# Fixed program order, phases, quadrant attention, DMA transposes and a Strassen second matmul in a sigmoid-attention + SiLU feed-forward kernel

## The chip, the cores and the metric

The kernel runs on one core of a Trainium2 chip. The metric is the time of one execution in microseconds (us) of the device. All quoted times are medians over the fast executions of a kernel (values_serial has one execution, of unknown state). Each kernel was run beside the kernel before on the same chip, and a ratio is the mean time of one kernel's fast runs over that of the kernel before's fast runs of the same rounds, so it is not quite the ratio of the medians quoted beside it. Experiments ran in four groups on four chips, so between groups the ratios are compared, not the times.

Short names: TensorE (PE in the profile) does matmuls, DVE is the vector engine, ACT the scalar engine (here: sigmoids), Pool is GpSimd, SP issues DMAs. SBUF is the on-chip memory, PSUM holds the results of matmuls, in banks. "Granted clock" is the share of full TensorE speed that the profile reports.

## The reference

Sigmoid attention for 8 batches of 12 heads (448 tokens, 64 values per head), followed by a two-matmul feed-forward block with SiLU over all 3584 tokens. Inputs and outputs are float32; both kernels multiply in float16.

```
q, k, v: (8, 12, 448, 64)   w_in: (768, 2048)   w_out: (2048, 768)
scores = q @ k^T / sqrt(64) - log(448)
x      = sigmoid(scores) @ v             # (8, 12, 448, 64) -> (3584, 768)
h      = x @ w_in                        # "first product"
out    = (h * sigmoid(h)) @ w_out        # "second product"
```

## The kernel before

It interleaves finely. For each pair of heads of batch b it issues the transposes of q and k on TensorE, four score blocks with their sigmoids and the values of the previous pair, and then one sixth of the feed-forward work of batch b - 1. A scheduler then orders the instructions; PSUM tiles come from two rotating pools. These are the parts that the change touches (cuts are marked):

```python
    def attention_part1(b: int, hp: int):
        # ... casting DMA loads of q16, k16, v16 (float32 -> float16) by the Pool queue ...
        for tsel, tin in ((0, q16), (1, k16)):
            ptr = ps_1.tile([P, 512], F32, ...)
            for c in range(NCH):            # 4 chunks of 112 tokens
                for j in range(2):          # 2 heads
                    nc.tensor.matmul(ptr[j*D:(j+1)*D, c*CP:(c+1)*CP],
                                     tin[:, j, c, :], ident[:CP, :CP], ...)   # a transpose, L94
            nc.vector.tensor_copy(qkT[:, tsel, :], ptr[:, :S])
        for c in range(NCH):
            # ... two score matmuls (one per head), one sigmoid, L107 and L114 ...

    def moe_out_unit(m, g):                 # second product: 128 tokens, L176
        for nh in range(2):                 # 2 x 384 output columns
            for fc in range(NFC - 1, -1, -1):        # 16 blocks of the inner dimension
                nc.tensor.matmul(po[:, :NO2], gTr[:, fc, g*P:(g+1)*P],
                                 w_out_sb[:, fc, nh*NO2:(nh+1)*NO2], ...)
            # ... DVE evacuates po with a scale into osb ...

    for b in range(B):
        for hp in range(NPAIR):
            va = attention_part1(b, hp)
            # ... values of the previous pair; some weights loaded ...
            if b > 0:
                moe_slice(b - 1, hp)        # a sixth of batch b-1's feed-forward work
```

## Time and profile before

| What | Before |
|---|---|
| Time, 3 runs | 490.87 us (490.77 to 491.74) |
| TensorE busy | 459.4 us of the span of 492.7 us of the profiled execution |
| First product (768 matmuls of 448 columns) | 1.14 us for six: 146 us |
| Second product (896 matmuls of 384 columns) | 2.60 us for sixteen: 146 us |
| Two transposes per head pair | 0.39 us each (median), 48 pairs |

From the profile page of the kernel before, four rows: busy microseconds with the share of the span and the number of instructions per engine; TensorE's busy tenths in 40 equal slices; the granted TensorE clock in tenths; and the shares of the chain of waits that ended last.

```profile
PE 459.4 (93%) x3200; PEld 227.7 (46%) x3200; DVE 184.1 (37%) x328; ACT 243.4 (49%) x321; POOL 124.7 (25%) x159
PE   3879999999999999999999999999999999999896
PEclk9985999999999999999999999999999999999999
PE 63%; ACT 25%; DVE 6%; DMA 2%; issue 2%; POOL 0%; ACTq 0%; POOLq 0%
```

A nine means 90% or more. From the fifth slice on (each is 12.3 us; the fourth is busy, but at a clock of 0.5) TensorE has work nearly all the time at full clock, and no other engine is busy for even half of the span. So the kernel is bound by the amount of work on TensorE, and only less work there, or denser work, can make it faster. ACT's quarter of the chain does not speak against it: TensorE's own waits for ACT add up to 6.8 us in the whole run.

The timeline of TensorE in the middle of the run prices that work. Columns: start, duration in us, engine, source line, operation, output and inputs, array tile, shapes, number of instructions, and in brackets the idle time before with what ended it.

```profile
231.21 0.39 PE L94 MATMUL ptr_2_0_2430<-ident,q_4_2_2423 112*64 112x112 f16 x8
231.55 0.39 PE L94 MATMUL ptr_2_1_2440<-ident,k_4_2_2424 112*64 112x112 f16 x8
232.32 0.96 PE L128 MATMUL pav_1_2467<-attnT_1_2356,v_4_1_2331 112*64 112x448 f16 x8 [0.38 <-DVE gTr L167]
235.75 0.40 PE L107 MATMUL psc_2_2_2459<-qkT_2_2429 64*112 64x448 f16 x2
236.08 0.55 PE L158 MATMUL ph_9_2487<-xT,w_in_sb 128*128 128x448 f16 x2
```

The first two lines are the two transposes of a head pair, 0.7 us together. `64*112` in the fourth line is the part of the 128x128 array that a score matmul uses, less than half of it; the two heads of a pair use the two halves. In the single records the two matmuls of a pair start 0.003 to 0.005 us apart. That line also shows a lone score pair amid the first product.

The chain of waits in order of time (start, duration, engine, tile, line) gives the pace and the ends:

```profile
171.09 2.42 ACT attnT_1_1758 L114 x3
286.47 2.42 ACT attnT_1_2992 L114 x3
448.00 1.29 PE ph_0_4713 L158 x6
```

The same tile of two later batches comes 115.4 us apart: 57.7 us per batch. The last batch's products begin at 448.0 us, with no attention beside them, and take the 44.7 us to the end of the span.

### The profile page before, as it was taken

The numbers are of one execution on the slowest core, as the hardware profiler recorded it, in microseconds if no ns is written. First come the engines' busy times: TensorE is split into PE (matmuls) and PEld (weight loads), VectorE is DVE, ScalarE is ACT, GpSimd is POOL, SyncE is SP. The second block draws the span as 40 slices with busy tenths as digits, with TensorE's granted clock in tenths as the row PEclk, the third lists the DMA queues.
The fourth block names the chain that finished last, engine by engine and source line by source line (L and its number), as shares of the span: only waits on it lengthen the run. The fifth ranks groups of instructions, "written<-read, shape, count | busy, mean of one in ns | idle before, by whom it ended". The sixth has DMA issues, their size and how long they took to land.

```text
span 492.7 us, 7595 instructions
## 1 busy us (share of the span) xinstructions
PE 459.4 (93%) x3200; PEld 227.7 (46%) x3200; DVE 184.1 (37%) x328; ACT 243.4 (49%) x321; POOL 124.7 (25%) x159
## 2 busy tenths in 40 slices
PE   3879999999999999999999999999999999999896
PEld 1333444544455444554455544454445544454463
DVE  2221453343622435226342353523533335324511
ACT  3665656347633575535743357427662275732400
POOL 9364231132301313113211131303321123000000
PEclk9985999999999999999999999999999999999999
DMA  9999975658456776764846666559483486211011
GB/s 89 168 169 189 179 51 37 92 63 55 29 60 93 72 45 44 73 93 31 55 29 93 92 46 41 60 64 85 30 57 75 83 57 39 18 59 40 0 56 73
DMA packets 140641, 34.30 MB, mean 70 GB/s; under 512 B 131904, under 2 KB 137024, under 8 KB 140608
## 3 DMA queue, kind: packets, MB, share of 16 engines
q0 software_dynamic: 136576, 22.82, 60.4%
q1 hardware_dynamic: 4032, 11.01, 5.9%
q8 instruction: 25, 0.41, 0.4%
q14 instruction: 8, 0.07, 0.0%
HBM read 45.61 MB, written 11.01 MB: 115 GB/s over the span
## 4 chain that ended last, share of the span: by engine, by line
PE 63%; ACT 25%; DVE 6%; DMA 2%; issue 2%; POOL 0%; ACTq 0%; POOLq 0%
DVE gTr L167 4%; DMA q_0_5_344<-in_q_dram 2%; ACT attnT_0_108 L114 1%; ACT attnT_1_1122 L114 1%; ACT attnT_1_2992 L114 1%; ACT attnT_1_4226 L114 1%; ACT attnT_1_2356 L114 1%; ACT attnT_1_1758 L114 1%; ACT attnT_1_3590 L114 1%; ACT attnT_1_521 L114 1%; DMA k_0_0_82<-in_k_dram 1%; PE pav_0_169 L128 1%; PE pav_4_388 L128 1%; PE po_3_0_4874 L176 1%; PE po_6_1_5006 L176 1%
## 5 line engine op out<-in xcount | busy, mean ns | idle before, releaser
L176 PEld LDWEIGHTS <-gTr 128*128 128x128 f16 x896 | 83.0, 98 | 68.3 <-issue 12.9
L158 PEld LDWEIGHTS <-w_in_sb 128*128 128x128 f16 x768 | 67.0, 98 | 81.2 <-issue 30.6
L114 ACT ACTIVATE attnT_0_2898<-psc_0_0_2899,bias_s 112x896 f16<-112x896 f32 x1 | 1.0, 1008 | 9.7 <-PE psc_0_0_2899 L107 9.7
L114 ACT ACTIVATE attnT_0_1028<-psc_0_0_1029,bias_s 112x896 f16<-112x896 f32 x1 | 1.0, 1008 | 9.7 <-PE psc_0_0_1029 L107 9.7
L114 ACT ACTIVATE attnT_0_1664<-psc_0_0_1665,bias_s 112x896 f16<-112x896 f32 x1 | 1.0, 1007 | 9.7 <-PE psc_0_0_1665 L107 9.7
L114 ACT ACTIVATE attnT_0_3496<-psc_0_0_3497,bias_s 112x896 f16<-112x896 f32 x1 | 1.0, 1007 | 9.7 <-PE psc_0_0_3497 L107 9.7
L114 ACT ACTIVATE attnT_0_2262<-psc_0_0_2263,bias_s 112x896 f16<-112x896 f32 x1 | 1.0, 1007 | 9.7 <-PE psc_0_0_2263 L107 9.7
L114 ACT ACTIVATE attnT_0_4132<-psc_0_0_4133,bias_s 112x896 f16<-112x896 f32 x1 | 1.0, 1007 | 9.7 <-PE psc_0_0_4133 L107 9.7
L114 ACT ACTIVATE attnT_5_1534<-psc_5_0_1535,bias_s 112x896 f16<-112x896 f32 x1 | 1.0, 1007 | 9.6 <-PE psc_5_0_1535 L107 9.6
L114 ACT ACTIVATE attnT_5_2768<-psc_5_0_2769,bias_s 112x896 f16<-112x896 f32 x1 | 1.0, 1007 | 9.6 <-PE psc_5_0_2769 L107 9.6
L114 ACT ACTIVATE attnT_5_4002<-psc_5_0_4003,bias_s 112x896 f16<-112x896 f32 x1 | 1.0, 1007 | 9.6 <-PE psc_5_0_4003 L107 9.6
L166 ACT ACTIVATE tsig_0_4720<-ph_0_4713 128x448 f16<-128x448 f32 x1 | 0.5, 544 | 10.5 <-PE ph_0_4713 L158 10.5
L114 ACT ACT_TABLE_LOAD x1 | 1.3, 1283 | 8.1 <-PE psc_0_0_109 L107 8.1
L94 PE MATMUL ptr_0_0_88<-ident,q_0_0_81 112*64 112x112 f16 x8 | 0.6, 299 | 4.6 <-DMA q_0_0_81<-in_q_dram 4.6
L176 PE MATMUL po_3_0_4874<-w_out_sb,gTr 128*128 128x384 f16 x16 | 2.8, 327 | 1.3 <-DVE gTr L167 1.3
L84 POOL DMA_DIRECT2D q_5_1_2965<-in_q_dram x1 | 0.8, 820 | 11.8 <-PE ptr_5_1_2758 L94 11.8
L84 POOL DMA_DIRECT2D q_7_1_4199<-in_q_dram x1 | 0.8, 820 | 11.8 <-PE ptr_5_1_3992 L94 11.8
L84 POOL DMA_DIRECT2D q_3_1_1731<-in_q_dram x1 | 0.8, 820 | 11.6 <-PE ptr_5_1_1524 L94 11.6
L84 POOL DMA_DIRECT2D q_6_2_3657<-in_q_dram x1 | 0.8, 820 | 11.4 <-PE ptr_0_1_3486 L94 11.4
L84 POOL DMA_DIRECT2D q_2_2_1189<-in_q_dram x1 | 0.8, 820 | 11.1 <-PE ptr_0_1_1018 L94 11.1
L84 POOL DMA_DIRECT2D q_3_2_1825<-in_q_dram x1 | 0.8, 820 | 11.1 <-PE ptr_0_1_1654 L94 11.1
L84 POOL DMA_DIRECT2D q_7_2_4293<-in_q_dram x1 | 0.8, 820 | 11.1 <-PE ptr_0_1_4122 L94 11.1
(1494 smaller groups left out, 1172.7 us busy)
## 6 DMA issues: line engine op xcount, KB each, us to landing
w_in_sb<-in_moe_w_in_dram POOLq DMA_DIRECT2D x4, 768.0 KB, 9.9
w_out_sb<-in_moe_w_out_dram POOLq DMA_DIRECT2D x4, 768.0 KB, 10.7
out_dram<-osb_0_833 SPq DMA_DIRECT2D x1, 384.0 KB, 2.9
out_dram<-osb_1_925 SPq DMA_DIRECT2D x1, 384.0 KB, 2.3
out_dram<-osb_2_963 SPq DMA_DIRECT2D x1, 384.0 KB, 2.4
out_dram<-osb_3_1431 SPq DMA_DIRECT2D x1, 384.0 KB, 2.3
out_dram<-osb_4_1469 SPq DMA_DIRECT2D x1, 384.0 KB, 2.4
out_dram<-osb_5_1561 SPq DMA_DIRECT2D x1, 384.0 KB, 2.3
```

The costliest lines, as they stand in the source:

```text
L84: nc.gpsimd.dma_start(t16.rearrange("p j c d -> p (j c) d"), tsrc[b, h0 : h0 + 2].rearrange("h (c p) d -> p (h c) d", p=CP),)
L94: nc.tensor.matmul(ptr[j * D : (j + 1) * D, c * CP : (c + 1) * CP], tin[:, j, c, :], ident[:CP, :CP], start=True, stop=True,)
L114: nc.scalar.activation(attnT[:, :, c, :], psc[:CP, :, :S], AF.Sigmoid, bias=bias_s[:CP], scale=QKSCALE,)
L128: nc.tensor.matmul(pav[j * D : (j + 1) * D, :S], v16[:, j, c, :], attnT[:, j, c, :], start=(c == NCH - 1), stop=(c == 0),)
L158: nc.tensor.matmul(ph[:, :S], w_in_sb[:, cc, fc * P : (fc + 1) * P], xT[:, cc, b * S : (b + 1) * S], start=(cc == NCC - 1), stop=(cc == 0),)
L166: nc.scalar.activation(tsig, ph[:, :S], AF.Sigmoid, bias=0.0, scale=ISX)
L167: nc.vector.tensor_mul(gTr[:, fc, (b % 2) * S : (b % 2) * S + S], ph[:, :S], tsig)
L176: nc.tensor.matmul(po[:, :NO2], gTr[:, fc, g * P : (g + 1) * P], w_out_sb[:, fc, nh * NO2 : (nh + 1) * NO2], start=(fc == NFC - 1), stop=( ...
```

## The change

Its intent: less TensorE work, and a program order and buffers fixed by hand so that what remains is dense.

- **Fixed order, phases.** No scheduler. Per batch, the first product runs alone over all eight PSUM banks (three pairs `att`, two singles `ffp`). Then the second product runs on the two `ffp` banks, and in nine "visits" the next batch's attention (up to three steps each) is put between its matmuls on the three `att` pairs.
- **Quadrants.** Four heads form a "quad". A score or value step is four matmuls, each on a 64x64 quadrant of the array: seven score and seven value steps per quad, three quads per batch. The seven value steps of a quad are issued together, as a "value group".
- **Transposes by DMA** from float16 copies (which Pool casts) from batch 1 on; batch 0 still uses TensorE.
- **Strassen (Winograd's form) for the second product**: per 256 tokens seven products of eight matmuls instead of 64 matmuls, paid for with sums on DVE: four over the weights once, four over the activations per 256 tokens, and three snapshots of PSUM.

A batch of 448 tokens has 1.75 such pairs of 128-token blocks, so batches 0 and 4 have a phase with one pair, the others phases with two. The core of the diff (long, cut; everything marked `+` is new):

```diff
-    # scheduler orders; ps_sc, ps_1 pools rotate
+    ctx.enter_context(tc.manual_schedule())
+    att = [psum.tile([P, 2, 512], F32, ...) for i in range(3)]
+    ffp = [psum.tile([P, 512], F32, ...) for i in range(2)]

+    def w_out_sums():                                # once; needs all of w_out (L91-L94)
+        nc.vector.tensor_sub(wt[:, 0], B12A, b11)
+        nc.vector.tensor_sub(wt[:, 1], b22, wt[:, 0])
+        nc.vector.tensor_sub(wt[:, 2], b21, wt[:, 1])
+        nc.vector.tensor_sub(B12A, b22, B12A)

-                    nc.tensor.matmul(ptr[...], tin[:, j, c, :], ident[:CP, :CP], ...)
+        nc.sync.dma_start_transpose(qkT[(b * NQ + n) % 3][kind], o.rearrange("p r i d -> p (r i d)"))

+    def values(b, n, pair):                          # L181; score_step (L161) is alike
+        for r in range(R):                           # 7 steps, quadrants (i, j) inside
+            for i, j in ((0, 0), (1, 1), (0, 1), (1, 0)):
+                nc.tensor.matmul(att[pair][i*HP:(i+1)*HP, j, :S],
+                                 vt[rj, i, r, :], attnT[rj, s0 + i, :],
+                                 start=(r == 0), stop=(r == R - 1))

+    def ff2_pair(m):                                 # 256 tokens, 7 x 8 matmuls (L272)
+        nc.vector.tensor_add(gs[:, 0], a21, a22)     # L259
+        nc.vector.tensor_sub(gs[:, 1], gs[:, 0], a11)
+        nc.vector.tensor_sub(gs[:, 3], a12, gs[:, 1])
+        nc.vector.tensor_sub(gs[:, 2], a11, a21)     # L262
+        yield from prod(X, a11, B11, True, False)
+        copy(0, X)                                   # DVE snapshot of PSUM, L283
+        yield from prod(Z, s1, T1, True, False)
+        copy(1, Z)
+        yield from prod(X, s2, T2, False, False)     # goes on in the bank that copy(0) reads
+        # ... four more products, combinations, stores ...

+    # ... batch 0's attention, loads and weights; loads and transposes of batch 1 ...
+    w_out_sums()
+    for b in range(B):
+        ff1(b)                                       # alone, L228; DVE multiplies (L241, L244)
+        # ... vs = the next batch's 21 score steps and 3 value groups in nine visits ...
+        for vi, us in enumerate(vs):
+            while done < (total - 12) * vi // (len(vs) - 1):
+                next(it); done += 1                  # a matmul of the second product
+            visit(us)
```

## The prediction

> **What bounds the kernel now.** TensorE. The page gives it 459 of 492.7 us (93%) and 63% of the chain of waits (ACT 25%). From 50 us on, the TensorE row of the 40 slices is nearly all nines at full clock; attention of batch 0 alone lasts until 46 us. The timeline prices the work: six 448-column matmuls of the first product take 1.14 us (768: 146 us); sixteen 384-column matmuls of the second take 2.60 us (896: 146 us); per head pair two transposes of up to 0.4 us, four score pairs of about 0.2 us plus switching, one value group of 0.9 us. A lone score pair inside the first product costs about 0.53 us where 0.19 streams: 0.34 us to switch in and out.
>
> **What the change does.**
> - Transposes leave TensorE for DMA (batch 0 excepted): 25 to 35 us less.
> - Strassen: 784 matmuls of 384 columns instead of 896: 127 us, 18 us less.
> - Attention in 64x64 quadrants: per batch 21 score and 21 value steps of four matmuls. The Trainium skill, "TensorEngine Tiling (Array Packing)", Key Properties, says that tiles run independently and that a mode change drains the array. The trace agrees for two tiles[...]; no run shows four. I take 0.2 us a step: 8.4 us a batch.
> - Added on DVE: sums for Strassen (estimate 0.65 us each, four per pair), snapshots and combinations (0.55 us, as in the trace). About 6 us per pair, beside 9 us of TensorE.
> - Moved: the first product now runs alone (18.2 us a batch), attention of the next batch only beside the second product, in nine visits.
>
> **Sum by stage (estimates from those durations).**
> - Attention of batch 0: first sigmoid near 11 us, 21 sigmoids at 0.92 us (the trace's spacing), copies, values at half clock: ends near 37 us.
> - First product of batch 0: half fits in eight banks, then it waits, since the Strassen weight sums stand before its multiplications on DVE and need all of w_out. At the 190 GB/s after casting of the slices near 50 us, w_out lands near 54 us, sums end near 60, the stage near 71 us.
> - Seven first products: 18.5 us each, 130 us.
> - Attention with two pairs (batches 1, 2, 3, 5, 6): 18.2 us second product + 8.4 us attention + 8 x 0.34 us switches + about 2.5 us waits = 32 us; 160 us.
> - With one pair (batches 0, 4): ACT-bound, 21 x 0.92 us plus values and waits, 27 us; 54 us.
> - Last second product, alone, with store: 23 us.
>
> Total about 438 us, range 418 to 466. Nearly all of the TensorE saving is on the critical path; some 15 us are lost again in the start-up stall, 2 to 3 us per phase at the borders.
>
> **What would show it.** TensorE idle near 47 to 60 us, released by DVE's weight sums, which wait for w_out's DMA. First-product phases of 18 to 19 us at full clock. Score steps near 0.2 us, value groups near 1.4 us. Two-pair phases near 32 us on TensorE, one-pair near 27 us on ACT.
>
> **What would make it wrong.** If only two quadrants run together, each two-pair phase grows by up to 8 us, the total nears 480. If DMA transposes are slow or wait behind stores on their queue, phases wait for transposed q and k. If w_out lands earlier, some 10 us are won.
>
> Chances: faster by over 2% 0.92, within 2% 0.05, slower 0.03.

## The result and the profile after

After: **431.78 us** (430.02 to 432.31, four runs) against 490.9 us (490.77 to 491.74) on the same chip: ratio 0.8787 (95% interval 0.8754 to 0.8819). The outputs were correct. The predicted 438 us was 1.4% high. The profiled execution has a span of 427.9 us.

The same rows of the page for the kernel after, with the DMA transposes' row (count; median us from issue to landing) at the end:

```profile
PE 380.4 (89%) x2948; PEld 192.2 (45%) x2948; DVE 196.0 (46%) x269; ACT 222.2 (52%) x256; POOL 75.6 (18%) x87
PE   5566825989999999999999999899999999999894
PEclk8566675999999999999999999999999999999998
PE 70%; DVE 10%; DMA 9%; ACT 7%; issue 1%; POOL 1%; SPq 0%; DVEq 0%; ACTq 0%; POOLq 0%
qkT<-st SPq DMA_TRANSPOSE x42, 3.2
```

TensorE's work fell by 79 us and the time by 59. The difference shows in the first eight slices (each 10.7 us): before, they were full from the fourth on, now there are fives and sixes, a 2 in the sixth, and a low clock. DMA and DVE hold 9 to 10% of the chain each, where they had 2% and 6%.

A fixed program order makes the stages easy to cut apart. This is the table by window for the kernel after: the first product of batch 0, a later first product, a phase with two pairs, one with one pair, and the last second product. Columns: the length, busy us of each engine with the number of instructions, granted clock, DMA share and GB/s.

```profile
core 0: us, PE busy (x) PEld busy (x) DVE busy (x) ACT busy (x) POOL busy (x), PEclk, DMA share, GB/s
44.97:80.40 35.43, 22.54 (x96) 10.40 (x95) 14.47 (x13) 7.03 (x9) 8.78 (x8) 0.74 1.04 206
103.65:121.75 18.10, 18.10 (x97) 9.29 (x95) 8.24 (x10) 7.14 (x9) 4.35 (x5) 1.00 0.74 173
121.90:151.25 29.35, 28.55 (x282) 14.73 (x282) 16.36 (x26) 20.18 (x22) 3.74 (x4) 1.00 0.61 122
264.60:287.90 23.30, 20.48 (x226) 9.91 (x226) 10.14 (x15) 19.63 (x22) 4.68 (x5) 1.00 0.72 151
400.90:427.90 27.00, 19.04 (x113) 10.67 (x111) 13.73 (x24) 0.54 (x1) 0.00 (x0) 0.94 0.22 59
```

Beside the prediction's sum, in us:

| Stage | Predicted | Measured | Error of the whole sum |
|---|---|---|---|
| Attention of batch 0, ends | 37 | 45.0 | +8.0 |
| First product of batch 0 | 34 | 35.4 | +1.4 |
| Seven other first products, each | 18.5 | 18.1 | -2.8 |
| Five two-pair phases, each | 32 | 29.35 | -13.2 |
| Two one-pair phases, each | 27 | 23.3 | -7.4 |
| Last second product and store | 23 | 27.0 | +4.0 |

The total was right to 10 us because +13 at the two ends met -23 in the middle. The middle is not one large error: it is a small one repeated. So the closeness of the total is in part luck.

The timeline of the start-up, all engines, in the kernel after:

```profile
12.32 6.40 ACT L171 ACTIVATE attnT<-att,bias_s 128x896 f16<-128x896 f32 x7
24.25 6.40 ACT L171 ACTIVATE attnT<-att,bias_s 128x896 f16<-128x896 f32 x7 [2.82 <-PE att L161]
35.33 6.40 ACT L171 ACTIVATE attnT<-att,bias_s 128x896 f16<-128x896 f32 x7 [2.72 <-PE att L161]
44.97 9.15 PE L228 MATMUL att<-xT,w_in_sb 128*128 128x448 f16 x36 [1.26 <-DVE xT L188]
52.81 1.76 DVE L91 TENSOR_TENSOR wt<-w_out_sb 128x3072 f16<-128x3072 f16 x1 [7.89 <-DMA w_out_sb<-in_moe_w_out_dram]
63.01 1.76 DVE L92 TENSOR_TENSOR wt<-w_out_sb,wt 128x3072 f16<-128x3072 f16 x1 [8.44 <-DMA w_out_sb<-in_moe_w_out_dram]
68.15 3.22 DVE L244 TENSOR_TENSOR gT<-att,tsig 128x896 f16<-128x896 f32 x3
69.29 8.94 PE L228 MATMUL att<-xT,w_in_sb 128*128 128x448 f16 x36 [12.89 <-DVE gT L244]
```

Read the last line first: TensorE was idle for 12.89 us until a multiplication on DVE (L244) let a bank go. That multiplication, at 68.15, stands behind the weight sums (L91 to L94) in DVE's order, and the second sum began at 63.01 because DVE waited 8.44 us for w_out. So the name in the bracket is DVE, but the cause is a DMA two steps back. The stall cost more than its 12.9 us: in the single records the first eleven intervals between matmuls after it are some 0.37 us and the later ones 0.19 (granted clock 0.50 from 69.3 to 73.3 us, 1.00 after), which is another 2.0 us. The first three lines show the other loss: seven sigmoids run without a gap from 24.25 to 30.65, and then ACT has none until 35.33. That hole of 4.7 us is the border between two quads: TensorE transposes, two engines copy, and a value group of 2.83 us at half clock (0.50) comes before the next scores. The border before it left a hole of 5.5 us (18.72 to 24.25).

The timeline of TensorE in a two-pair phase of the kernel after:

```profile
130.96 1.52 PE L181 MATMUL att<-attnT,v 64*64 64x448 f16 x28
134.59 0.49 PE L272 MATMUL ffp<-wt,gT 128*128 128x384 f16 x2
135.01 0.76 PE L161 MATMUL att<-qkT,qkT 64*64 64x448 f16 x12
135.70 1.15 PE L272 MATMUL ffp<-wt,gT 128*128 128x384 f16 x6
```

Twenty-eight value matmuls on quadrants take 1.52 us; in the single records, four start within 0.01 us, the next four 0.21 us later, and from then on four every 0.19 us. Twelve score matmuls sit between matmuls of the second product. In the single records the last of these starts at 134.753 and the first score matmul at 135.009, 0.26 us later where 0.16 is the spacing inside the second product: 0.09 us to switch in. The last score step starts at 135.41 and the second product again at 135.70, 0.29 instead of 0.19: 0.10 us to switch out. Together 0.19 us, where the prediction had 0.34.

What TensorE waited for over the whole run of the kernel after (us in total, times, longest):

```profile
PE att L228 <- DVE gT L244: 12.9, 1, 12.9
PE att L161 <- ACT attnT L171: 10.0, 21, 1.7
PE ffp L272 <- DVE snap L283: 3.1, 7, 1.0
```

The third line is mostly a matter of the last stage. Its timeline in the kernel after, DVE and TensorE:

```profile
402.23 0.69 DVE L259 TENSOR_TENSOR gs<-gT 128x1024 f16<-128x1024 f16 x1
404.29 0.68 DVE L262 TENSOR_TENSOR gs<-gT 128x1024 f16<-128x1024 f16 x1
404.89 1.01 DVE L283 TENSOR_SCALAR snap<-ffp 128x384 f32<-128x384 f32 x2
405.50 1.46 PE L272 MATMUL ffp<-wt,gs 128*128 128x384 f16 x8 [1.04 <-DVE snap L283]
```

The first product of Strassen's seven is done early, but its snapshot stands behind all four activation sums, and TensorE may not go on in that bank before.

### The profile page after: what moved, and what is told of

Same layout as the page of the kernel before. It is cut to its first block, busy times and chain, and to the rows that moved or that the text cites. A ratio compares the mean times of both kernels' runs of the same rounds, so it can differ in the third digit from the quotient of the medians.

```text
span 427.9 us, 7184 instructions
## 1 busy us (share of the span) xinstructions
PE 380.4 (89%) x2948; PEld 192.2 (45%) x2948; DVE 196.0 (46%) x269; ACT 222.2 (52%) x256; POOL 75.6 (18%) x87
## 4 chain that ended last, share of the span: by engine, by line
PE 70%; DVE 10%; DMA 9%; ACT 7%; issue 1%; POOL 1%; SPq 0%; DVEq 0%; ACTq 0%; POOLq 0%
PE att L228 24%; PE ffp L272 24%; DMA w_out_sb<-in_moe_w_out_dram 8%; PE ffp L228 8%; PE att L181 8%; ACT attnT L171 5%; PE att L161 5%; DVE gs L260 1%; DVE gs L261 1%; DVE gs L259 1%; DVE gs L262 1%; DMA st<-in_k_dram 1%; ACT tsig L239 1%; DVE snap L283 1%; DVE osb L308 1%
## 5 line engine op out<-in xcount | busy, mean ns | idle before, releaser
L171 ACT ACTIVATE attnT<-att,bias_s 128x896 f16<-128x896 f32 x168 | 156.1, 1012 | 33.4 <-PE att L161 33.1
L228 PE MATMUL att<-xT,w_in_sb 128*128 128x448 f16 x576 | 115.7, 361 | 14.2 <-DVE gT L244 12.9
L243 ACT ACTIVATE tsig<-att 128x896 f16<-128x896 f32 x48 | 44.0, 917 | 122.2 <-PE att L228 105.7
L244 DVE TENSOR_TENSOR gT<-att,tsig 128x896 f16<-128x896 f32 x48 | 52.3, 1091 | 70.4 <-ACT tsig L243 70.3
L121 POOL CAST st<-st 128x896 f16<-128x896 f32 x48 | 46.3, 965 | 172.5 <-DMA st<-in_q_dram 120.7
L161 PE MATMUL att<-qkT,qkT 64*64 64x448 f16 x672 | 51.8, 375 | 11.6 <-ACT attnT L171 10.0
L272 PEld LDWEIGHTS <-gs 128*128 128x128 f16 x448 | 40.4, 98 | 41.1 <-issue 16.5
L272 PE MATMUL ffp<-wt,gs 128*128 128x384 f16 x224 | 43.0, 327 | 3.4 <-DVE snap L283 3.1
L272 PE MATMUL ffp<-w_out_sb,gT 128*128 128x384 f16 x224 | 43.4, 327 | 2.8 <-DVE gT L241 2.8
L272 PEld LDWEIGHTS <-gT 128*128 128x128 f16 x336 | 31.0, 98 | 29.5 <-issue 11.2
L181 PE MATMUL att<-attnT,v 64*64 64x448 f16 x672 | 40.4, 380 | 2.7 <-ACT attnT L171 1.7
L272 PE MATMUL ffp<-w_out_sb,gs 128*128 128x384 f16 x224 | 42.3, 327 | 0.0
L117 POOL CAST v<-st 128x896 f16<-128x896 f32 x24 | 22.5, 936 | 94.3 <-PE att L181 72.9
L286 DVE SCALAR_TENSOR_TENSOR osb<-ffp,snap 128x384 f32<-128x384 f32 x42 | 23.3, 555 | 33.2 <-PE ffp L272 33.2
L161 PEld LDWEIGHTS <-qkT 64*64 64x64 f16 x672 | 19.2, 108 | 41.0 <-issue 34.7
L181 PEld LDWEIGHTS <-v 64*64 64x64 f16 x672 | 20.1, 113 | 19.5 <-issue 9.7
```

The costliest lines, as they stand in the source:

```text
L117: nc.gpsimd.tensor_copy(o.rearrange("p i r d -> p i (r d)"), t)
L121: nc.gpsimd.tensor_copy(o.rearrange("p r i d -> p i r d"), t.rearrange("p i (r d) -> p i r d", r=R))
L161: nc.tensor.matmul(att[pair][cj, i, :S], kT[ri, r, cj], qT[ri, :, cj], start=True, stop=True,)
L171: nc.scalar.activation(attnT[:, s0 : s0 + 2, :], att[pair][:, :, :S], AF.Sigmoid, bias=bias_s, scale=QKSCALE)
L181: nc.tensor.matmul(att[pair][i * HP : (i + 1) * HP, j, :S], vt[rj, i, r, :], attnT[rj, s0 + i, :], start=(r == 0), stop=(r == R - 1),)
L228: nc.tensor.matmul(o, w_in_sb[:, cc, f * P : (f + 1) * P], xT[:, cc, :], start=(cc == 0), stop=(cc == NCC - 1),)
```

## The experiments

The theory from the trace: the phases are as cheap as they are because transposes left TensorE, quadrants run four at a time, and switches are cheap; the start-up is expensive because the weight sums stand too early in DVE's order and w_out comes late. Its rivals: the stall at the start is only the first of two limits, and removing it moves the wait into the next phase; Strassen's smaller count of matmuls is what pays; the phases owe their time to the fixed order, and the quadrants or the transposes matter little. Every experiment gave correct outputs, and all but one were timed in four runs.

| Run | Time, us | Ratio to before (95%) |
|---|---|---|
| after (for comparison) | 431.78 | 0.8787 (0.8754 to 0.8819) |
| sums_late | 420.81 | 0.8555 (0.8498 to 0.8612) |
| plain_second | 420.47 | 0.8559 (0.8512 to 0.8606) |
| loads_after_w_out | 419.73 | 0.8533 (0.8479 to 0.8586) |
| both | 422.27 | 0.8593 (0.8549 to 0.8637) |
| values_serial (one run, state unknown) | 467.73 | - |
| one_step_visits | 447.65 | 0.9103 (0.9050 to 0.9155) |
| pe_transposes | 478.99 | 0.9746 (0.9678 to 0.9815) |
| tuned | 412.97 | 0.8406 (0.8351 to 0.8462) |
| tuned2 | 415.94 | 0.8443 (0.8396 to 0.8491) |
| tuned2_plain | 426.27 | 0.8666 (0.8621 to 0.8710) |
| tuned3 | 408.36 | 0.8319 (0.8257 to 0.8381) |

The kernel before had medians of 492.44 us beside the first four experiments, 493.04 beside the next four (one of these seven executions was slow, and the ratios leave it out), 493.04 beside tuned2 and tuned2_plain, and 490.6 beside tuned3.

### sums_late: the weight sums after the first product of batch 0

```diff
-    w_out_sums()
     for b in range(B):
         ff1(b)
+        if b == 0:
+            w_out_sums()
```

> The four Strassen weight sums come after the first product of batch 0 in program order, nothing else changes. Theory 1 (the start-up wait is made by their place in DVE's order): the 13 us hole in TensorE near 57 to 69 us goes, the first first-product phase ends near 65 us instead of 80, w_out still lands near 63 us, the sums run at 65 to 72, the second product of batch 0 waits some 2 to 4 us for them; total about 418 to 421 us against 431.8. Theory 2 (the start-up is bound by the arrival of w_out, the order only shows it): the wait moves into the phase after, which grows from 23 to over 32 us; total 428 us or more.

Measured: the first product of batch 0 took 20.1 us (44.6 to 64.7) instead of 35.4, but the one-pair phase behind it 30.8 us instead of 23.3. From TensorE's waits in sums_late:

```profile
PE ffp L272 <- DVE gs L259: 6.8, 2, 6.6
```

One wait of 6.6 us has taken the place of the one of 12.9: the second product needs the activation sums, which now stand on DVE behind the weight sums (65.9 to 74.2 us). So moving the sums took 15.3 us out of one stage and put 7.5 back into the next. The program order was half of the stall; the other half moved on, as the rival had it, though it is not w_out's arrival that binds there but DVE's time for the sums (8.3 us).

### plain_second: no Strassen at all

```diff
-        nc.vector.tensor_add(gs[:, 0], a21, a22)
-        # ... sums, seven products, snapshots, combinations ...
+        for t in range(2):
+            for nh in range(2):
+                for fc in range(NFC):
+                    nc.tensor.matmul(bank, gT[:, fc, c:c+P],
+                                     w_out_sb[:, fc, nh*EH:(nh+1)*EH],
+                                     start=fc == 0, stop=fc == NFC - 1)
+                    yield
+                nc.vector.tensor_scalar_mul(o[:, nh*EH:(nh+1)*EH], bank, ISX)
-    w_out_sums()
-        total = (hi - lo) * 56
+        total = (hi - lo) * 64
```

> The second product without Strassen: 64 matmuls per 256 tokens instead of 56, no weight sums, no activation sums, no snapshots; phases, attention and buffers unchanged. If TensorE's work decides everywhere: 14 x 8 x 0.1625 us = 18 us slower. Theory 1 says the start-up hole (13 us) goes with the weight sums, the last phase loses its waits (27 us less 19 us busy, so about -3 net of 2.6 more matmul time), two-pair phases grow by 2.6 us each (5 x), one-pair phases by at most 1 us: about 426 to 432 us, so Strassen as placed wins nothing net.

Measured: 112 more matmuls, and yet 11 us faster than the kernel after. The first product of batch 0 took 20.0 us; each two-pair phase 30.8 to 30.9 us. Its table by window, for the phase of batch 1, with the same columns as above:

```profile
105.60:136.40 30.80, 30.80 (x298) 16.16 (x298) 8.20 (x12) 20.18 (x22) 5.49 (x6) 1.00 0.66 142
```

TensorE is busy for all of it, where the kernel after has 28.55 of 29.35. So Strassen's sixteen saved matmuls per two-pair phase, 2.6 us of streaming (16 x 0.163 us), are worth 1.5 us there, and the sums at the start cost 15. As placed in this change, Strassen loses 11 us, more than the expectation had (426 to 432 us), since the two-pair phases grew by 1.5 us and not by 2.6. The rival that its smaller count is what pays is refuted.

### loads_after_w_out: batch 1's loads wait for w_out

A tiny Pool copy from w_out's last block into the buffer of batch 1's first load (below called the gate) makes that load, and those behind it on the queue, wait until w_out has landed. The load overwrites the copied values, so the result stays correct.

```diff
+    nc.gpsimd.tensor_copy(st32[n32[0] % 5][:, 0, 0:2], w_out_sb[:, NFC - 1, 0:2])
     for i in range(NQ, NQ + 3):
         prep(i)
         stage(i)
     w_out_sums()
```

> The loads of batch 1 are held until the last piece of w_out has landed (a two-element copy of it into the first load's buffer), sums stay where they were. If w_out is late because it shares the DMA engines with batch 1's loads and transposes (4.1 MB and 1.4 MB): w_out lands near 52 us instead of 63, the hole shrinks by some 9 to 11 us; total about 421 us. If w_out is late for another reason (its own rate): landing stays within 3 us of 63, total unchanged or worse by the later loads.

From DVE's timeline in loads_after_w_out, the sum that needs the last of w_out:

```profile
50.96 1.76 DVE L92 TENSOR_TENSOR wt<-w_out_sb,wt 128x3072 f16<-128x3072 f16 x1 [5.54 <-DMA w_out_sb<-in_moe_w_out_dram]
```

It started 12.0 us earlier (63.01 before the edit). The first product of batch 0 ended at 68.2 instead of 80.4 us; the phase behind it grew by 1.5 us. So the lateness of w_out in the kernel after is shared DMA, not the weights' own size: alone, the rest of the weights moved at 192 GB/s after casting (24.7 to 51.0 us), which is 384 GB/s of float32 source bytes. The Trainium skill, "DMA: Bandwidth & Descriptors", Specifications, gives about 358 GB/s per core, as half of what two cores share; this kernel runs on one core, and its measured rate is above that share. The prediction's 190 GB/s after casting (380 GB/s of source) was a fair reading of the whole rate; the mistake was to give all of it to w_out.

### both: the two edits together

```diff
+    nc.gpsimd.tensor_copy(st32[n32[0] % 5][:, 0, 0:2], w_out_sb[:, NFC - 1, 0:2])
-    w_out_sums()
+        if b == 0:
+            w_out_sums()
```

> Sums late and loads held, together. Theory 1 with shared DMA: first-product phase ends near 65 us, sums wait for nothing but DVE, the phase after keeps about 23 to 27 us; total about 415 to 418 us, a few us better than sums_late alone. If batch 1's q and k then come too late, the attention phase waits for them at its start and both is no better than sums_late.

Measured: no better than either alone, and 4 us above what was expected. w_out landed at 51 us again, but the sums stand behind the first product's multiplications and ran from 65.4 to 74.2. Batch 1's casts on Pool fell into the same time, in sums_late as well as here. From the timeline of both, DVE and Pool:

```profile
67.07 1.45 POOL L121 CAST st<-st 128x896 f16<-128x896 f32 x1 [0.96 <-PE att L161]
67.76 2.37 DVE L92 TENSOR_TENSOR wt<-w_out_sb,wt 128x3072 f16<-128x3072 f16 x1
68.87 2.04 POOL L117 CAST v<-st 128x896 f16<-128x896 f32 x1 [0.36 <-DMA st<-in_v_dram]
```

The same sum took 1.76 us when Pool was quiet and takes 2.37 here; a cast of 0.94 us takes 1.45 and 2.04. The Trainium skill, "SBUF — State Buffer", Who interferes with whom, says that a DVE instruction with two SBUF inputs contends with a GpSimd instruction that reads SBUF. The trace agrees and gives the price above (in sums_late three casts took 1.92 to 2.24 us beside the sums). The three lines also show the two engines taking turns: the first cast ends at 68.52, the subtraction 1.61 us later (70.13), the second cast 0.78 us after that (70.91), each a little less than its quiet duration after the other's end. The two gains do not add, since with the sums behind the first product w_out's earlier arrival removes no wait: in sums_late, too, it had landed before they began.

### values_serial: the quadrants of a value group one after another

```diff
-        for r in range(R):
-            s0 = slot_of(b, n, r)
-            for i, j in ((0, 0), (1, 1), (0, 1), (1, 0)):
+        for i, j in ((0, 0), (1, 1), (0, 1), (1, 0)):
+            for r in range(R):
+                s0 = slot_of(b, n, r)
```

> The same 28 value matmuls per group, but all seven of one quadrant before the next, so neighbours in the program share a quadrant. If the gain of the quadrants comes from four neighbours in four different quadrants running together (the trace after shows four starts within 0.01 us, groups of 1.45 us): a group becomes serial, 28 x 0.187 = 5.2 us, two-pair phases grow by about 11 us each, batch 0's attention at half clock by about 20 us, total near 520 us. If TensorE overlaps quadrants whatever the order: group stays near 1.5 us and the total near 432 us.

Measured: 467.73 us in one run, two-pair phases of 34.8 us, one-pair phases of 29.0 us. So the order in which the four quadrants of the value groups are issued is worth some 5.4 us per phase (the scores were left as they are). Neither expected size of the value group came: from the first start to the last it took 2.95 us, not 5.2 (one quadrant at a time) and not 1.17 (four at a time, as in the kernel after). Per matmul that is 0.109 us (2.95 / 27), between one and two in flight. TensorE's timeline in values_serial at the end of a value group:

```profile
136.40 2.73 PE L181 MATMUL att<-attnT,v 64*64 64x448 f16 x25
138.79 0.38 PE L161 MATMUL att<-qkT,qkT 64*64 64x448 f16 x2
138.97 0.35 PE L181 MATMUL att<-attnT,v 64*64 64x448 f16 x1
138.98 0.38 PE L161 MATMUL att<-qkT,qkT 64*64 64x448 f16 x3
```

In program order all 28 value matmuls (L181) come before the score matmuls (L161). Here two score matmuls start at 138.79, and another value matmul starts at 138.97. So matmuls on different quadrants do not start in program order: a quadrant that is free takes its next matmul while another is still behind. In the single records each next quadrant starts right after the fourth of the seven matmuls on the one ahead (136.994 after 136.988). Why the fourth is not shown by any run; a short queue per quadrant would do it, but that is only argued.

### one_step_visits: 24 visits of one unit instead of nine of up to three

```diff
-                vs.append(us[:3])
-                us = us[3:]
+                vs.append(us[:1])
+                us = us[1:]
...
-                visit(us)
+                visit(us, vi % 3)
```

> Attention beside the second product in 24 visits of one unit instead of nine of up to three, the same work. My prediction charged 0.34 us per switch in and out (from a lone score pair of the kernel before); the trace after reads 0.19 us. At 0.19 us: 15 more switches add 2.8 us to each of five two-pair phases, one-pair phases (ACT-bound) about nothing or win, total near 445 us. At 0.34 us: 5.1 us each, total near 457 us. If switching cost nothing, finer interleaving would leave 431 us or less.

Measured: two-pair phases of 32.8 us (the first three; 32.2 the last two) instead of 29.5 by the same measure. Fifteen more visits cost 3.3 us: 0.22 us for each switch in and out. That agrees with the single records above (0.09 in, 0.10 out, and 0.02 us more for the first step of a visit). The one-pair phases (23.4 and 24.0 us instead of 23.4) hardly moved, for there ACT sets the pace. About 16 of the 18 us between the profiled spans (445.9 against 427.9) went into the five two-pair phases. Most of the rest lies at the start, which the edit does not touch: there TensorE's longest wait was 16.6 us instead of 12.9, and the first product of batch 0 ended at 82.2 instead of 80.4.

### pe_transposes: q and k transposed on TensorE again

```diff
+                if n == 0 and r == 0:
+                    o += [("t", b, 0, 0), ("t", b, 0, 1)]
+                if n < NQ - 1 and r == 4:
+                    o += [("t", b, n + 1, 0), ("t", b, n + 1, 1)]
...
+            if u[0] == "t":
+                pe_transpose(u[3], u[1], u[2], pair, "dve")
+                pair += 1
...
-                if kind < 2:
-                    dma_transpose(kind, *quads[i])
```

(`st16` gets eight buffers instead of four, since the casts must live longer.)

> From batch 1 on, q and k are transposed on TensorE again (42 matmuls of 128 columns a batch, evacuated by DVE), not by DMA. My prediction valued the transposes' leaving TensorE at 25 to 35 us. In this layout: 42 x 0.056 = 2.4 us plus about 4 switches and an evacuation wait at the phase's start, 4 to 5 us a phase, seven phases: 28 to 35 us slower in the steady part; w_out may land 1 to 3 us earlier, as 1.4 MB of transposes leave the DMA engines. Total 455 to 465 us. If the transposes were hidden anyway: within 5 us of 432.

Measured: 478.99 us (455 to 465 expected), 47 us slower than the kernel after by the ratios, and so close to the kernel before that faster by over 2% is not settled. The two-pair phases grew by 4.7 to 6.5 us, the one-pair phases by 4.5, about 39 us in all. TensorE's waits in pe_transposes show that a part of this is not streaming but copying:

```profile
PE att L161 <- DVE qkT L150: 16.3, 9, 2.2
```

Nine times scores waited, 16.3 us in all, for DVE to bring the transposed tiles out of PSUM, work that DMA transposes do not need. Two more visits per phase (11 instead of 9, since the transposes count as units of a visit) are in the sum, too; at some 0.2 us each (an estimate from one_step_visits) they make 3 us of the 39. The expectation for the start was wrong, too: w_out did not land earlier without the DMA transposes but later (72.9 us), and the first product of batch 0 ended 9.3 us later. In the kernel after, batch 1's later loads stand behind its transposes on the SP queue (issued from 52.4 us, the next loads at 59.7), and so reach the DMA engines late; without the transposes they ran beside the weights. In this layout, then, the DMA transposes are worth some 39 us in the steady phases, which was predicted as 25 to 35, and another 9 at the start by accident. With values_serial this refutes the last rival as it was put: neither the order of the quadrants (some 35 us, single run) nor the place of the transposes (47 us) matters little. What the fixed order is worth by itself no run shows, since none goes back to the scheduler; and these amounts hold in the new layout only and do not add up to the 59 us of the change.

### tuned: a version built from what was learned

Changes: the weight sums go one at a time behind the last four multiplications of the first product of batch 0; only batch 1's second and third quads are held back by the gate; batch 0's next transposes come a visit earlier, and its values after three score steps; two activation sums are put behind the first two snapshots.

The edit against the kernel after:

```diff
-    w_out_sums()
+    for u in range(4):
+        at(("f", 0, u + 4), weight_sums[u])
+        if i == NQ + 1:
+            nc.gpsimd.tensor_copy(st32[n32[0] % 5][:, 0, 0:2], w_out_sb[:, NFC - 1, 0:2])
-            us.insert(2, ("a", 0, n - 1))
+            us.insert(3, ("a", 0, n - 1))
+            if vi == 1 and n + 1 < NQ:
+                first(n + 1)
         copy(0, X)
+        nc.vector.tensor_sub(gs[:, 3], a12, gs[:, 1])
         # ... and gs[:, 2] behind copy(1, Z) ...
```

> A candidate that puts the findings together: weight sums one at a time between the multiplications of the first product of batch 0, loads of batch 1 from its second quad on held until w_out has landed, batch 0's transposes issued a visit earlier and its values after three score steps instead of two, activation sums interleaved with the snapshots. Batch 0's attention ends near 39 us instead of 45, its first product near 60 instead of 80, two-pair phases 29 us, the last stage 25 us instead of 27: total near 407 us. If the sums' arrival still binds (w_out after 55 us), about 412 us.

Measured: 412.97 us. Attention of batch 0 ended at 39.3 (45.0 before), its first product took 18.3 us, the last product's matmuls 18.8 us instead of 21.2, and two-pair phases 29.1 and 28.7. But the first phase took 33.2 us: w_out landed only at 58.6, and everything behind the weight sums on DVE waited for it; scores, too, waited up to 2.7 us for transposed q and k that the gate had held back.

### tuned2 and tuned2_plain: hold all loads back, with and without Strassen

tuned2 sets the gate ahead of all of batch 1's loads and starts the second product 24 matmuls earlier than the first visit; tuned2_plain is tuned2 with the plain second product. The edit against tuned:

```diff
-        if i == NQ + 1:
-            # ... the gate ...
+    # gate ahead of all loads; then loads in the order in which they are cast
+    for kind, i in ahead[:5]:
+        load(kind, *quads[i])
-                target = (total - tail) * vi // (len(vs) - 1) if len(vs) > 1 else 0
+                pre = 24 if b == 0 else 0
+                target = pre + (total - tail - pre) * vi // (len(vs) - 1)
```

> The candidate once more: all loads of batch 1 held until w_out has landed (near 51 us), with the loads of the next quad issued before the transposes of the one before, and 24 matmuls of batch 0's second product ahead of its first attention visit. Batch 0's first product ends near 58 us with its weight sums done near 60; q and k of batch 1 ready near 62 us; that phase ends near 85 us instead of 91; total near 406 to 408 us. If the start is bound by the sum of bytes (weights plus the first quad of batch 1) whatever the order, the phase still ends near 90 us and the total stays near 412 us.

> The same start-up with the plain second product: what Strassen is worth where its sums cost nothing at the start. Two-pair phases 30.9 us against 29.1 (five), the last stage 2.2 us longer, one-pair phases about equal: 11 to 12 us slower than tuned2, so near 418 us. If Strassen's gain is eaten elsewhere too, the two are within 4 us of each other.

Measured: tuned2 missed. It is no faster than tuned (0.8443 against 0.8406, overlapping intervals); its first phase ended at 91.8 us, tuned's at 90.7. From its timeline, TensorE:

```profile
61.23 1.46 PE L271 MATMUL ffp<-w_out_sb,gT 128*128 128x384 f16 x8 [3.37 <-DVE gT L242]
64.76 1.51 PE L271 MATMUL ffp<-wt,gs 128*128 128x384 f16 x8 [2.08 <-DVE gs L260]
69.21 0.87 PE L162 MATMUL att<-qkT,qkT 64*64 64x448 f16 x12
```

w_out had landed at 50.6 us and the first transposed q and k of batch 1 by 65.1, but the scores (L162) began only at 69.21. They stand behind the 24 matmuls of the second product that the edit put first (L271), and these waited for multiplications and activation sums that stand on DVE behind and between the weight sums. From 69.76 on ACT ran all 21 sigmoids without a gap. So here the order of work held the phase back, and no longer the arrival of w_out; what holding back all loads is worth alone this run does not show. tuned2_plain gives the comparison of Strassen when its sums are well placed: 426.27 against 415.94 us, so Strassen wins 10 us (0.8666 against 0.8443). Of that, the five two-pair phases give 9.8 by the stage borders (30.9 us against 29.1 three times and 28.7 twice).

### tuned3: nothing held back, the weight sums inside the first phase

The gate is gone. The weight sums are issued after the first visits of batch 1's attention, one each, and batch 0's second product starts only after the fifth visit. The scores, which need only batch 1's data, go first while w_out is still landing. The edit against tuned:

```diff
-            nc.gpsimd.tensor_copy(st32[n32[0] % 5][:, 0, 0:2], w_out_sb[:, NFC - 1, 0:2])
-    for u in range(4):
-        at(("f", 0, u + 4), weight_sums[u])
+                late = 4 if b == 0 else 0
+                if b == 0 and 1 <= vi <= 4:
+                    weight_sums[vi - 1]()
+                target = max(0, (total - tail) * (vi - late) // (len(vs) - 1 - late))
```

> The candidate with nothing held back: batch 1's loads go beside the weights as in the change, the four weight sums and then the second product of batch 0 come only after the first attention visits of batch 1, which need neither. First product ends near 58 us, attention of batch 1 starts at once since its first quads are loaded by then, w_out lands near 63 us, sums end near 70 us behind attention; the phase is ACT-bound and ends at 84 to 87 us instead of 91 (tuned, tuned2); total near 406 to 409 us. If the bytes still bind, q and k of the second or third quad come late and the phase ends near 90 us, total near 412 us.

Measured: **408.36 us**, ratio 0.8319 (0.8257 to 0.8381), the fastest kernel and 5% below the kernel after by either measure (its interval just overlaps tuned's, so tuned3 over tuned is likely, not settled). Its first phase, in the table by window with the same columns:

```profile
59.50:86.80 27.30, 22.19 (x226) 10.74 (x226) 17.94 (x19) 19.85 (x22) 5.62 (x6) 0.87 1.13 194
```

It takes 27.3 us where the same phase elsewhere takes 23.3, so some 4 us of lateness are left there. The first product of batch 0 took 20.1 us against 18.3 in tuned; the 1.8 us are clock and not waiting: the first ten matmuls or so start 0.37 us apart (granted clock 0.56 from 39.5 to 43.5 us; 1.00 there in tuned). That product ends at 59.5 us instead of 80.4.

## Why the prediction was right or wrong, point by point

**Right: what bounds the kernel, and that nearly all of the saved work counts.** TensorE's busy time fell by 79 us (459.4 to 380.4) and the span by 65 (492.7 to 427.9); the prediction had some 15 us lost again.

**Right, undersized: transposes on DMA, "25 to 35 us less".** Undone in the new layout they cost some 39 us in the steady phases (pe_transposes). The estimate priced the matmuls only; the 16.3 us of waits for the copies out of PSUM, and two more visits per phase, came with them. The two amounts are not quite the same thing: the estimate is of transposes in the kernel before.

**Right: four quadrants at "0.2 us a step".** A value group of seven steps takes 1.52 us and a step streams in 0.19. The Trainium skill, "TensorEngine Tiling (Array Packing)", Key Properties, has tiles independent and the array drained at a mode change; the trace agrees with the first (28 matmuls started within 1.17 us, where one at a time, 0.19 us apart, they would need 5.3) and shows a cost at each mode change (0.09 and 0.10 us), though not that it is a drain. "TensorE: Matmul & The Clock Gate", Measured speedup vs the span model, adds about 4 ns per further tile to one matmul's duration; here four starts lie 3 to 4 ns apart (135.009, .012, .015, .019).

**Wrong in size: "8 x 0.34 us switches + about 2.5 us waits".** A switch in and out costs 0.19 to 0.22 us (single records, one_step_visits), and TensorE's idle time in a two-pair phase is 0.8 us (29.35 less 28.55 busy). The sum with measured terms: 18.3 (112 matmuls at 0.163) + 7.9 (42 steps at 0.189) + 1.9 (nine visits at about 0.21) + 0.8 = 28.9; 0.5 us of the 29.35 is not assigned. The 0.34 was read from lone score pairs in the kernel before, and did not carry over to groups of steps.

**Wrong in size: "ACT-bound, 21 x 0.92 us plus values and waits, 27 us".** The bound is right: ACT is busy 19.6 of 23.3 us. The allowance of nearly 8 us for the rest was twice the measured 3.7.

**Right: "first-product phases of 18 to 19 us" (18.1), and, in mechanism, the stall at the start.** The stall was named with its cause, "TensorE idle near 47 to 60 us, released by DVE's weight sums, which wait for w_out's DMA". It came from 56.4 to 69.3 us, 12.9 us long, and made that stage longer by 15.3 us (sums_late; the rest is mostly the low clock after it), where "some 15 us are lost again" was said. Only its place in time was off, by two terms: **"ends near 37 us"** for batch 0's attention, which was 45.0, since ACT's row of sigmoids, which the sum took as unbroken, breaks for 5.5 and 4.7 us at the two borders between quads (tuned and tuned3 took 5.5 us of this away by issuing the transposes earlier); and **"w_out lands near 54 us"**, which was 63.0, because batch 1's loads share the DMA (loads_after_w_out: 51.0 when they do not).

**Right: "some 10 us are won" if w_out lands earlier** (loads_after_w_out: 12 us). **Not seen:** that Strassen as a whole is a loss here, 18 us of streaming saved and more than that spent. The term "Strassen ... 18 us less" was worth about 10 us once the sums were well placed, and less than nothing in the change itself. Of the 18, 13 lie in the five two-pair phases, which gained 9.8: a part came back as idle time of TensorE (0.8 us a phase in the kernel after, none in plain_second). The one-pair phases, bound by ACT, gained only 0.3 us each (by their borders in plain_second).

**Wrong in size: the last product, "23 us".** It took 27.0. Its 112 matmuls stream in 18.3 us but took 21.2, since snapshots stand behind activation sums (tuned, which interleaves them: 18.8), and from the last matmul (422.6) to the end of the span it was 5.3 us more.

**Still open.** What the fixed order is worth without the rest. Why a next quadrant in values_serial starts after the fourth matmul of the one ahead. How the 9 us between w_out's predicted and measured landing split into shared bandwidth and order of issue. Why one_step_visits waited 3.7 us longer at the start than the kernel after, with the same instructions there. By spans of the profiled runs sums_late gains 8.5 us, by the ratios 11: the executions of the kernel after spread over 2.3 us, and the profiled one was its fastest.

## What to carry to other kernels

Price a change stage by stage: a sum can be right while its parts err by +13 and -23 us, as here, and the parts are what the next version is built from. A saving in matmuls that needs sums on another engine is worth what that engine's program order allows: put each sum just behind the last thing that must not wait for it, and start with work that does not need the late data. Mixing array modes was cheap here in groups of three steps (0.2 us a visit); issue quadrants round-robin, not one after another.

## What the Trainium skill lacked or had wrong

- "TensorE: Matmul & The Clock Gate", Part 3, What overlaps and what doesn't, calls matmuls "pc-monotone in start AND end — strict FIFO, no reordering", and "PSUM — Partial Sum Buffer", Engine vs sequencer instructions, says that they start and complete in program order. In values_serial two score matmuls start at 138.79 us, ahead of a value matmul (138.97) that comes before them in the program: between quadrants the starts were not in program order.
- "TensorEngine Tiling (Array Packing)", Key Properties, says that a mode change drains the array but gives no cost. Here it was 0.09 us in and 0.10 us out, 0.22 us per extra visit.
- The same page says nothing of the order of issue that four quadrants need. Round-robin ran 28 matmuls in 1.17 us from the first start to the last, seven in a row on each quadrant in 2.95 us.
- "DMA: Bandwidth & Descriptors", Latency and other measured facts, gives DMA transposes a bandwidth (261 GB/s in one kernel) but no time from issue to landing. Here the median for the 224 KB of a transpose was 3.2 us, with other traffic beside it.
- "SBUF — State Buffer", Who interferes with whom, calls the shared port pair an exclusive lock, and gives no price for a DVE instruction with two SBUF inputs. The runs agree with the lock (the engines take turns, see the run both) and show the price: 1.76 us became up to 2.48 for a DVE subtraction, 0.94 up to 2.24 for a cast on Pool (sums_late).
